# Attention and a gated expert product on one core: where unread products stand, and how late a scheduler takes results for TensorE to be

## The chip, the cores and the metric

One core of a Trainium2 chip runs the whole program in one launch. The metric is the time of one execution on the device in microseconds (us), as the median of the runs shown. Five instruction queues run beside each other: TensorE (PE in the profile; its weight loads are PEld), VectorE (DVE), ScalarE (ACT), GpSimd (POOL) and SyncE (SP), which here issues all transfers. Each queue runs its instructions in the order in which the program lists them, and waits on semaphores for what the others make.

## What is computed

The reference, cut to its core (8 batches, 8 heads, 576 positions, 64 columns of a head; d_model 512, d_ff 2048):

```python
scores = scale * q @ k.T + (cum[:, None] - cum[None, :])   # cum: running sum of log f
scores = where(causal, -1e9, scores)
attn = exp(scores - scores.max(-1)); attn /= attn.sum(-1) + 1e-9
x = (attn @ v)                       # heads side by side: 4608 tokens x 512
h = x @ w_in
g = h * tanh(softplus(h))
out = g @ w_out
```

## The kernel before

All products run with fp16 operands that are split into a high and a low part, so that one product of the reference becomes two or three on TensorE (some products of the first attention pairs run in fp32).

**Attention** goes by 32 pairs of heads, four pairs to a batch. For each pair the two operands are loaded (`qk`), scaled and split on DVE and ACT (`hl`), sent by transfers into the tiles `st1` and `st2` from which TensorE reads them, and multiplied. The first eight pairs take the row maxima first: TensorE writes scores, DVE reduces them (`mx`), the maxima are rounded (`m16`), turned on TensorE against the identity (`idh`), copied (`mr`) and sent back into `st1` as one more row. Later pairs (`new_st_items`) write scores into a bank of PSUM, DVE takes the minimum of the negated scores (`mn`), ACT takes the exponential (`st<-b,mn`), the result is split (`hb`) and turned by a transfer (`pt<-hb`), and TensorE multiplies it with the values (`b<-vv,pt`); DVE divides (`rr`, then `x<-b,rr`), splits (`xp`) and a transfer turns that into `xa`.

**Experts** go by nine chunks of 512 tokens. For each chunk TensorE forms `b<-xa,wall` (192 products of 512 columns), ACT applies the gate (`me`), DVE and ACT split it (`gh`, `gl`), and TensorE forms `b<-gh,wall` and `b<-gl,wall` (192 more). Chunk c needs the whole of batch c; the ninth chunk holds the last 64 positions of all batches. So there are 3456 products with `wall`, 384 to a chunk, and they are TensorE's filler beside the attention of the next batch. PSUM has eight banks, `b0` to `b7`. Before the experts start, attention uses all but one; from then on it has two alone (`NA = 2`, lines 909 and 1598), `b0` and `b1`, and every use of a bank waits until the last reader of the one before has left it.

**The order** of all instructions is written by a planner in the kernel's own code (class `Program`, lines 109 to 465 and on). `add` and `choose` record each operation with what it reads and writes and a cost. `schedule` (line 306) runs `forward` (line 367) ten times, each with ranks from `backward`, and keeps the order with the earliest modelled end; `emit` (line 293) writes that order out, queue by queue. `forward` is a list scheduler: it keeps a clock for each queue, takes the queue that can go first, picks the operation with the best rank whose inputs have arrived by the model, and sets when its results arrive at others: its end plus a fixed delay of its queue:

```python
DELAY = {"tensor": 197, "vector": 140, "scalar": 150, "gpsimd": 80}
```

The maps `read` and `written` hold, bank by bank, when the last reader or writer leaves it by the model. Nothing of these model times is in the program that runs: only the order is.

`forward` also places **unread products**: 128x128 products of the identity with itself into a spare part of `b7` (`emit`, the branch `i < 0`), which nothing reads. They occupy TensorE in its early gaps, so that the activity that sets its clock goes on. They are placed while `filling` holds, which ends with the first product that has `wall` as its weights. In the profile they are the line L299, `b<-idh`.

Of the kernel before, what the change touches and what calls it, by code (L numbers as in the profile page):

```python
# [26 lines left out]
P = 128  # L27
# [16 lines left out]
STAY = 10000.0  # L44
TICK = 10240.0 / 3.0
WARM = 3072.0
IDLE = 300.0
MAN = "PE"
PLO0 = ("T00", "T20", "T01", "T21",)
# [95 lines left out]
class Program:  # L145
# [221 lines left out]
    def forward(self, deps, succ, rank):  # L367
        ops = self.ops
# [5 lines left out]
        clock = {q: 0.0 for q in self.NAMES}  # L374
# [8 lines left out]
        left, half, mode = {}, 0, False  # L383

        def arrive(i):
            for o, (q, _, _, _) in enumerate(ops[i][0]):
                heappush(coming[q], (ready[i], i, o))
# [19 lines left out]
        order = []  # L407

        read, written = {}, {}
        filling, began, fills = True, False, 0  # L410
        while len(order) < n + fills:
            clock["sync"] = max(clock["sync"], hw, dma - BACK)
            best = None
            for q in self.NAMES:
# [5 lines left out]
                if r or c:  # L420
                    t = clock[q] if r else max(clock[q], c[0][0])
                    if best is None or (t, q) < best:
                        best = (t, q)
            t, q = best
# [7 lines left out]
            while ripe[q]:  # L432
# [3 lines left out]
                late = max([other.get(b, 0.0) for b in self.banks[x[1]]], default=0.0)  # L436
# [38 lines left out]
            if wait:  # L475
                heappush(ripe[q], got)
                _, i, o, t = min(wait)
# [3 lines left out]
            if way[0][1].startswith("dma_start"):  # L481
                hw = max(t, hw) + cost[0]
                clock[q] = t + 50
                dma = max(dma, hw + 650) + cost[1]
                end, own = dma + 930, 0.0
            else:
                if q == "tensor":
                    filling = filling and ops[i][0][o][1][0][3].get("lhsT", self.idle[1]).tensor.name != self.last
                    e = clock[q]
                    while filling and began and t - e > IDLE:  # L490
                        k = int((e + 197.0) / TICK)
                        e += P / (2.4 if left.get(int(e / TICK) - 1, 0.0) >= WARM else 1.2) + 2.5
                        left[k] = left.get(k, 0.0) + P
                        order.append((-1, 0))
                        fills += 1
                    began = True
                    t = max(t, e)
                    cols, weight, h, m = cost
                    if m != mode:
                        t += 97.0  # L500
                    mode = m
                    slow = 1.0 if left.get(int(t / TICK) - 1, 0.0) >= WARM else 2.0
                    cost = 22.0 if h and half and h != half else cols * slow / 2.4 + (2.5 if slow < 2 else 0.0)
                    a, b = (t + 197.0) / TICK, (t + 197.0 + cols * slow / 2.4) / TICK
                    for k in range(int(a), int(b) + 1):
                        left[k] = left.get(k, 0.0) + weight * (min(b, k + 1) - max(a, k)) / (b - a)
                    half = h
                elif lock:
                    port = max(t, port) + cost
                    cost = port - t  # L510
                elif q == "scalar" and self.sets[i] not in (None, table):
                    table = self.sets[i]
                    cost += 1370.0
                clock[q] = t + cost
                end, own = clock[q], self.DELAY[q]
            ends[i] = end
            for b in self.banks[i]:
                (written if q == "tensor" else read)[b] = end + own
            for j in succ[i]:
                d = 0.0 if q == "tensor" and ops[j][0][0][0] == q else own  # L520
                ready[j] = max(ready[j], end + d)
                need[j] -= 1
                if not need[j]:
                    arrive(j)
# [1145 lines left out]
```

## Time and profile before

| | |
|---|---|
| median of 3 runs | 1052.54 us (1052.1 to 1053.11) |
| the profiled execution | 1052.55 us, its span 1050.8 us |
| PE busy | 1009.3 us (96%), 7404 instructions |
| DVE busy | 712.9 us (68%) |
| ACT busy | 644.5 us (61%) |
| mean granted TensorE clock | 0.996 of full speed |
| DMA | 140.12 MB |

The profile is of one execution. Busy times are of instructions that do work; a waiting engine is idle. A row of the timeline gives start, length, engine, operation and tiles, how many instructions were merged, and in brackets the engine's idle time before it and what ended it. Nearly all instructions are recorded through one helper and carry its line, L302, so groups are told apart by the names of their tiles. A product of 512 columns is listed with the time from its start to its modelled end; the next one starts before that.

### The profile page before, as it was taken

To read this page: it belongs to the slowest core of one execution; us is meant where nothing else is said; L and a number is where in the kernel's file an instruction comes from. 1 tells how busy PE (TensorE), PEld (TensorE's weight loads), DVE (VectorE), ACT (ScalarE), POOL (GpSimd) and SP (SyncE) were. 2 spreads that over 40 slices of the span, in tenths; PEclk is the share of its full clock that TensorE was granted. 3 is DMA by queue.
4 is the path that set the end of the run, shared out by engine and by line. 5 is a ranking of instruction groups with operands and counts; after the bars stand their busy time and mean duration, and the time that the engine had idled before them with its cause. 6 is when DMAs were issued, how large, how long until landed. Compare 5 with 4: busy or idle time off the path is not lost.

```text
span 1050.8 us, 19908 instructions
## 1 busy us (share of the span) xinstructions
PE 1009.3 (96%) x7404; PEld 541.9 (52%) x7404; DVE 712.9 (68%) x1965; ACT 644.5 (61%) x1160; POOL 13.7 (1%) x63
## 2 busy tenths in 40 slices
PE   2899999999999999999999999999999999999998
PEld 2787566554445545445545554554455554444443
DVE  6799999867777877777777786777776663121211
ACT  5367887556777867777777767777676573112111
POOL 3000000000000000000000000000000000000000
PEclk9899999999999999999999999999999999999999
DMA  8698856548685877586767666766556332000001
GB/s 281 179 248 233 251 153 177 186 104 189 129 164 128 189 144 151 120 185 147 133 143 177 139 146 134 160 150 125 117 131 131 76 64 65 1 1 30 11 1 41
DMA packets 239340, 140.12 MB, mean 133 GB/s; under 512 B 206885, under 2 KB 207665, under 8 KB 239242
## 3 DMA queue, kind: packets, MB, share of 16 engines
q1 hardware_dynamic: 239242, 138.84, 56.9%
q8 instruction: 58, 0.95, 0.4%
q14 instruction: 40, 0.33, 0.1%
HBM read 48.33 MB, written 12.57 MB: 58 GB/s over the span
## 4 chain that ended last, share of the span: by engine, by line
PE 67%; DVE 12%; ACT 11%; DMA 5%; issue 4%; SPq 1%; ACTq 0%; POOL 0%; DVEq 0%
PE b L302 66%; ACT L302 3%; DMA st<-hl 3%; ACT st L302 2%; DVE b L302 2%; ACT hb L302 2%; ACT junk L302 2%; DVE vv L302 2%; DVE hb L302 1%; DVE hl L302 1%; ACT me L302 1%; DVE x L302 1%; DVE mx L302 1%; SPq L302 1%; DMA v<-in_v_dram 1%
## 5 line engine op out<-in xcount | busy, mean ns | idle before, releaser
L302 PEld LDWEIGHTS <-wall 128*128 128x128 f16 x3456 | 330.4, 98 | 374.6 <-issue 1.5
L302 PE MATMUL b<-xa,wall 128*128 128x512 f16 x1728 | 408.6, 379 | 0.0
L302 PE MATMUL b<-gh,wall 128*128 128x512 f16 x1152 | 356.8, 379 | 0.0
L302 PE MATMUL b<-gl,wall 128*128 128x512 f16 x576 | 218.3, 379 | 0.0
L302 ACT ACTIVATE st<-b,mn 128x512 f32<-128x512 f32 (+3 forms) x240 | 115.3, 524 | 102.1 <-DVE mn L302 90.4
L302 ACT ACTIVATE me<-b,cinv 128x512 f32<-128x512 f32 x144 | 93.1, 685 | 125.2 <-PE b L302 124.5
L302 DVE TENSOR_SCALAR gh<-me,gsc 128x512 f16<-128x512 f32 x135 | 63.7, 484 | 144.1 <-ACT me L302 140.9
L302 PE MATMUL b<-st 70*128 70x256 f16 (+12 forms) x1008 | 145.0, 278 | 12.3 <-DVE x L302 5.2
L302 ACT ACT_TABLE_LOAD x110 | 141.1, 1283 | 9.5 <-DVE mn L302 5.9
L302 DVE TENSOR_TENSOR hb<-st,hb 128x512 f16<-128x512 f32 x144 | 98.7, 690 | 62.7 <-ACT hb L302 61.9
L302 PE MATMUL b<-vv,pt 128*128 128x65 f16 (+4 forms) x2464 | 122.3, 208 | 5.7 <-ACT st L302 4.2
L302 PEld LDWEIGHTS <-st 70*128 70x128 f16 (+5 forms) x1008 | 77.4, 101 | 74.5 <-issue 33.8
L302 DVE CUSTOM_DVE_ANT_0 b<-b,mskw 128x512 f32<-128x512 f32 (+1 forms) x192 | 94.3, 499 | 27.3 <-PE b L302 21.9
L302 DVE SCALAR_TENSOR_TENSOR gl<-me,gsc,gh 128x512 f16<-128x512 f32 x144 | 102.2, 746 | 0.0
L302 ACT ACTIVATE hb<-st 128x512 f16<-128x512 f32 x144 | 89.3, 628 | 11.5 <-DMA pt<-hb 10.1
L302 PEld LDWEIGHTS <-pt 128*128 128x128 f16 (+1 forms) x2016 | 61.4, 101 | 20.4 <-issue 7.2
L302 ACT ACTIVATE junk<-qk 128x576 bf16<-128x576 f32 x64 | 43.5, 680 | 16.5 <-DMA qk<-in_qk_dram 15.6
L302 PEld LDWEIGHTS b<-vv,pt 128*128 128x128 f32 (+1 forms) x448 | 51.1, 183 | 4.5 <-issue 1.3
L302 DVE SCALAR_TENSOR_TENSOR hl<-qk,qt,hl 128x576 f16<-128x576 f32 x64 | 50.6, 810 | 0.0
L302 DVE SCALAR_TENSOR_TENSOR wall<-wall 128x512 int32<-128x512 int32 x64 | 43.1, 679 | 0.0
L302 ACT ACTIVATE xp<-x 128x128 f16<-128x128 f32 (+1 forms) x40 | 15.6, 418 | 44.0 <-DVE x L302 44.0
L302 DVE TENSOR_REDUCE mx<-b 128x1 f32<-128x384 f32 (+5 forms) x72 | 34.1, 511 | 11.9 <-PE b L302 11.7
(105 smaller groups left out, 639.1 us busy)
## 6 DMA issues: line engine op xcount, KB each, us to landing
st<-hl SPq DMA_DIRECT2D x192, 144.0 KB
qk<-in_qk_dram SPq DMA_DIRECT2D x32, 576.0 KB
v<-in_v_dram SPq DMA_DIRECT2D x32, 288.0 KB
out_dram<-ot SPq DMA_DIRECT2D x36, 256.0 KB
wall<-in_w_in_dram SPq DMA_DIRECT2D x16, 512.0 KB
wall<-in_w_out_dram SPq DMA_DIRECT2D x16, 512.0 KB
pt<-hb SPq DMA_TRANSPOSE x144
part<-ot SPq DMA_DIRECT2D x8, 256.0 KB
```

Source lines behind the costliest of these rows:

```text
L302: r = getattr(real[eng], method)(*a, **kw)
```

## The change

Two things change in `forward`, and a constant `SLACK = 600.0` (nanoseconds) is added.

First, the unread products. Before, the operation that ended a gap was appended to the order and the unread products that were to fill the gap were appended after it. Now they are inserted in front of it. The filling also stops early: past the middle of a gap, once the clock is full by the model and the activity counted so far is enough by its reckoning.

Second, once the experts run (`filling` is off), whatever VectorE, ScalarE, GpSimd or a transfer makes for TensorE, and every bank that VectorE or ScalarE has read, is taken by the model to come 600 ns later than before. Results for other engines keep their times, and so does TensorE's own work.

```diff
--- before.py
+++ after.py
@@ -44,6 +44,7 @@
 STAY = 10000.0
 TICK = 10240.0 / 3.0
 WARM = 3072.0
+SLACK = 600.0
 IDLE = 300.0
 MAN = "PE"
 PLO0 = ("T00", "T20", "T01", "T21",)
@@ -486,12 +487,17 @@
             else:
                 if q == "tensor":
                     filling = filling and ops[i][0][o][1][0][3].get("lhsT", self.idle[1]).tensor.name != self.last
-                    e = clock[q]
-                    while filling and began and t - e > IDLE:
+                    e, full = clock[q], t - IDLE
+                    while filling and began and e < full:
                         k = int((e + 197.0) / TICK)
-                        e += P / (2.4 if left.get(int(e / TICK) - 1, 0.0) >= WARM else 1.2) + 2.5
+                        warm = left.get(int(e / TICK) - 1, 0.0) >= WARM
+                        now = int((t + 197.0) / TICK)
+                        due = 1.2 * WARM * ((t + 197.0) / TICK - now)
+                        if warm and 2.0 * e > clock[q] + t and left.get(now, 0.0) > due:
+                            break
+                        e += P / (2.4 if warm else 1.2) + 2.5
                         left[k] = left.get(k, 0.0) + P
-                        order.append((-1, 0))
+                        order.insert(-1, (-1, 0))
                         fills += 1
                     began = True
                     t = max(t, e)
@@ -514,10 +520,12 @@
                 clock[q] = t + cost
                 end, own = clock[q], self.DELAY[q]
             ends[i] = end
+            late = 0.0 if q == "tensor" or filling else SLACK
             for b in self.banks[i]:
-                (written if q == "tensor" else read)[b] = end + own
+                (written if q == "tensor" else read)[b] = end + own + late
             for j in succ[i]:
-                d = 0.0 if q == "tensor" and ops[j][0][0][0] == q else own
+                to = ops[j][0][0][0]
+                d = 0.0 if q == to == "tensor" else own + late if to == "tensor" else own
                 ready[j] = max(ready[j], end + d)
                 need[j] -= 1
                 if not need[j]:
```

The new order places 164 unread products where there were 182, and otherwise the same 6967 products. Here is how it moves instructions at two places on PE.

**Place 1: PE, the end of pair 0's maxima and the begin of pair 1's.** `b2<-idh,m16` is the turn of pair 0's maxima, `b4<-st1_1` the first score product of pair 1. Before (78 unread products stand between the turn and that product, 35 more behind it):

```order
L302 MATMUL b1_0_116<-msk2_77,idm_75 128x64
L302 LDWEIGHTS m16_0_126
L302 MATMUL b2_0_118<-idh_74,m16_0_126 9x128
L299 LDWEIGHTS idh_74
L299 MATMUL b7_0_105<-idh_74 128x128
...
L302 LDWEIGHTS st1_1_82
L302 MATMUL b4_0_120<-st1_1_82 128x128
L299 LDWEIGHTS idh_74
L299 MATMUL b7_0_105<-idh_74 128x128
...
L302 LDWEIGHTS idm_75
L302 MATMUL b4_0_120<-msk_76,idm_75 128x128
```

In the change (58 stand in front of the turn, the last two of them shown; 26 between it and the product):

```order
L300 LDWEIGHTS idh_74
L300 MATMUL b7_0_105<-idh_74 128x128
L303 LDWEIGHTS m16_0_126
L303 MATMUL b2_0_118<-idh_74,m16_0_126 9x128
L300 LDWEIGHTS idh_74
L300 MATMUL b7_0_105<-idh_74 128x128
...
L303 LDWEIGHTS st1_1_82
L303 MATMUL b4_0_120<-st1_1_82 128x128
L303 LDWEIGHTS idm_75
L303 MATMUL b4_0_120<-msk_76,idm_75 128x128
```

So the gap's fill has moved ahead of the operation that waits, and behind pair 1's first product none is left. The first group of the program moves in the same way: 35 stood behind pair 0's first score product `b2<-st1_0` and now stand in front of it.

**Place 2: PE, a bank that goes from the product with the values to the scores of the next pair, in the third batch.** `b1<-vv,pt` are the last products with the values; the next user of `b1` is `b1<-st1_1 128x256`; products with `wall` stand between. Before (9 of them; the fence leaves out six):

```order
L302 MATMUL b1_0_116<-vv_0_128,pt_2_135 64x65
L302 LDWEIGHTS wall_69
L302 MATMUL b2_0_118<-xa1_87,wall_69 128x512
L302 LDWEIGHTS wall_69
L302 MATMUL b2_0_118<-xa1_87,wall_69 128x512
...
L302 LDWEIGHTS wall_69
L302 MATMUL b3_0_119<-xa1_87,wall_69 128x512
L302 LDWEIGHTS st1_1_82
L302 MATMUL b1_0_116<-st1_1_82 128x256
L302 LDWEIGHTS st2_1_85
```

In the change (14 of them):

```order
L303 MATMUL b1_0_116<-vv_0_128,pt_2_135 64x65
L303 LDWEIGHTS wall_69
L303 MATMUL b3_0_119<-xa1_87,wall_69 128x512
L303 LDWEIGHTS wall_69
L303 MATMUL b3_0_119<-xa1_87,wall_69 128x512
...
L303 LDWEIGHTS wall_69
L303 MATMUL b4_0_120<-gl_1_166,wall_69 128x512
L303 LDWEIGHTS st1_1_82
L303 MATMUL b1_0_116<-st1_1_82 128x256
L303 LDWEIGHTS st2_1_85
```

Five more products of 512 columns stand between the bank's last write and its next, and two of them are now from the second half of the experts.

## Rows read from the trace of the kernel before

**Rows 1.** The page's first part: busy time, share of the span, instructions.
```profile
PE 1009.3 (96%) x7404; PEld 541.9 (52%) x7404; DVE 712.9 (68%) x1965; ACT 644.5 (61%) x1160; POOL 13.7 (1%) x63
```

**Rows 2.** PE's waits in 0 to 98 us: total, times, longest us.
```profile
PE b L302 <- DVE am_m L302: 14.3, 1, 14.3
PE b L302 <- DVE m L302: 4.8, 1, 4.8
PE b L302 <- DMA st<-hl: 3.1, 1, 3.1
```

**Rows 3.** PE's waits in 98 to 1051 us, the same columns.
```profile
PE b L302 <- ACT st L302: 6.9, 14, 1.3
PE b L302 <- DVE x L302: 5.2, 10, 1.4
PE b L302 <- DMA pt<-hb: 0.6, 1, 0.6
PE b L302 <- ACT pt L302: 0.2, 1, 0.2
```

**Rows 4.** Timeline, 14 to 42 us, all queues, rows of several windows.
```profile
14.35 0.59 PE L302 MATMUL b<-am_m,ones 128*128 128x1 f32 x2 [14.35 <-DVE am_m L302]
14.62 3.92 SPq L302 DMA_DIRECT2D st<-hl  x6
18.01 0.26 PE L302 MATMUL b<-st 70*128 70x128 f16 x1 [3.07 <-DMA st<-hl]
18.07 3.94 PE L299 MATMUL b<-idh 128*128 128x128 f16 x35
...
21.31 0.77 ACT L302 ACTIVATE hl<-qk,qt 128x576 f16<-128x576 f32 x1 [1.65 <-DMA st<-hl]
21.80 0.30 PE L302 MATMUL b<-msk,idm 128*128 128x128 f16 x1
22.48 1.35 DVE L302 TENSOR_REDUCE mx<-b 128x4 f32<-128x512 f32 x3 [3.57 <-PE b L302]
23.75 0.51 DVE L302 TENSOR_SCALAR hl<-qk,qt 128x576 f16<-128x576 f32 x1
23.87 0.20 PE L302 MATMUL b<-msk,idm 128*128 128x64 f16 x1
24.33 4.43 SPq L302 DMA_DIRECT2D st<-hl  x6
28.62 0.18 DVE L302 TENSOR_SCALAR m<-mx 128x9 f16<-128x9 f32 x1
28.86 0.27 PE L302 MATMUL b<-idh,m 128*9 128x128 f16 x1 [4.78 <-DVE m L302]
29.06 6.01 PE L299 MATMUL b<-idh 128*128 128x128 f16 x78
31.14 0.69 DVE L302 SCALAR_TENSOR_TENSOR wall<-wall 128x512 int32<-128x512 int32 x1
34.97 2.12 PE L299 MATMUL b<-idh 128*128 128x128 f16 x35
36.92 0.22 PE L302 MATMUL b<-msk,idm 128*128 128x128 f16 x1
37.53 1.95 DVE L302 TENSOR_REDUCE mx<-b 128x4 f32<-128x512 f32 x4 [5.70 <-PE b L302]
```

**Rows 5.** Busy us by stretch: length, PE, PEld, DVE, ACT, POOL, granted clock, DMA share, GB/s.
```profile
24.20:28.90 4.70, 0.04 (x1) 0.04 (x1) 4.67 (x14) 0.35 (x2) 0.00 (x0) 0.62 0.77 212
24.10:38.90 14.80, 9.54 (x134) 9.18 (x135) 9.04 (x26) 1.84 (x5) 0.24 (x1) 0.77 0.70 218
38.90:100.20 61.30, 60.28 (x615) 49.70 (x615) 56.12 (x169) 39.82 (x91) 1.03 (x7) 1.00 0.84 217
```

**Rows 6.** Timeline of PE and DVE, 244 to 248 us (place 2).
```profile
244.15 2.12 PE L302 MATMUL b<-xa,wall 128*128 128x512 f16 x9
246.92 0.42 DVE L302 TENSOR_TENSOR x<-b,rr 128x256 f32<-128x256 f32 x1
247.26 0.34 DVE L302 TENSOR_SCALAR x<-b,rr 128x128 f32<-128x128 f32 x1
247.65 0.60 PE L302 MATMUL b<-st 70*128 70x256 f16 x4 [1.39 <-DVE x L302]
```

**Rows 7.** Instructions that write `b`: count, ns min/median/max, first and last start, forms.
```profile
L302 PE MATMUL b<-xa,wall x1728: 376/379/390, 100.2 to 1035.8; 128*128 128x512 f16 x192
```

**Rows 8.** Busy us by stretch, one batch and the end, columns as in rows 5.
```profile
425.00:534.00 109.00, 106.09 (x830) 54.17 (x830) 82.48 (x232) 80.40 (x144) 0.56 (x4) 1.00 0.72 150
857.00:1047.00 190.00, 189.56 (x955) 87.11 (x954) 47.58 (x91) 41.91 (x64) 0.00 (x0) 1.00 0.07 21
```

**Rows 9.** The chain that ended last, two of its pieces: start, length, what.
```profile
642.60 38.39 PE b L302 x340
...
856.95 189.63 PE b L302 x955
```

## Prediction, made before the changed kernel ran

> **What bounds the kernel now.** I read the page's first part first: PE is busy 96% of the span, DVE 68%, ACT 61% [rows 1]. The chain of waits agrees: it runs on PE alone for 38 us in the middle of a batch and for the last 190 us [rows 9]. So only time in which PE does no useful product can be won: the 41.5 us in which it is idle (1050.8 less 1009.3), and what the profile counts as busy although nobody reads it. The waits of PE divide the idle time. Before 98 us it waits three times for long: 14.3 us for its first operand, 3.1 us for a transfer, 4.8 us for the rounded maxima [rows 2]. After 98 us it waits 26 times, 12.9 us in all, mostly for an ACT or DVE operation that reads one of the two banks of attention [rows 3]. A wait costs more than its row says: a 512-column product is listed with 379 ns [rows 7], while nine of them in 2.12 us start (2.12 - 0.379)/8 = 0.218 us apart [rows 6]; so about 0.16 us of each wait lies under the end of the product before. 26 times 0.16 is 4.2 us, and the waits after 98 us cost about 17.1 us.
>
> **Part one, the unread products.** The timeline of the start shows what they do now [rows 4]. The first score product of pair 0 runs at 18.01, when its transfer has landed. Then come 35 unread products, to 21.80, and only then the rest of pair 0's scores, whose operand is the same tile. DVE sits idle 3.57 us for that. The turn of the maxima runs at 28.86, 78 unread products follow to 34.9, one score product of pair 1, then 35 more, to 36.92; DVE sits idle 5.70 us until 37.53. PE was not short of ready work: pair 1's operands were being sent from 24.33 on, and the first such transfer of pair 0, issued at 14.62 and needed at 18.01, took at most 3.4 us, so they were there by about 28.
>
> Step by step in the change. The first 35 start behind the product that ends at 14.94. At (3.94 - 0.25)/34 = 0.108 us each they end at 18.7, 0.7 us later than pair 0's operand arrives. The other 26 products of pair 0, which took from 21.80 to 24.07, then run from 18.75 to 21.0, 3.05 us sooner. DVE's three reductions move to about 19.4 and end by 20.8. Its next step, the split of pair 1, needs the buffer that transfers still read: ACT's half of that split started at 21.31 for that reason. So DVE's block from 23.75 to 28.80, 5.05 us all but without a gap [rows 4, 5], starts at 21.3 and ends at 26.35: 2.45 us sooner, not 3.05. Before the turn stand 58 unread products: at (2.12 - 0.22)/34 = 0.056 us each they need 3.2 us of the 5.3 us there, so they cost nothing; at 0.108 they would end at 27.3 and cost 0.9. Then 26 more, 1.5 us (2.8 at the lower clock). Pair 1's scores start at about 28 to 29.2 and go through without a break, where 36.92 was. DVE has 3.0 us of other work behind the maxima (28.80 to 31.83), so it reduces from about 29.5, not 37.53: **8 us** sooner.
>
> How much of that lasts? From 38.9 to 100.2 us PE is busy 60.28 of 61.3 us, DVE 56.12, transfers 0.84 [rows 5]: all three are nearly full, so each has to start this stretch sooner. PE and DVE can, by 8. The transfers between 24.1 and 38.9 are busy 0.70 of 14.8 us, so they have 4.4 us of idle time to give, and are issued 2.4 us sooner: 6.8. I take 6, and take off 0.5 us for three later groups, 12, 19 and 5 products, where 25 stood, if their gaps are not there on the chip (11 times 0.056). Sum -5.5; ends -2 (only the 2.45 us of the maxima, less the fills) and -9 (DVE's whole idle time, 3.57 and 5.70).
>
> The granted clock is 0.77 between 24.1 and 38.9 [rows 5], part of it at 1.2 GHz after the idle stretch ahead of 28.86. With 58 products in that stretch the lower level should be gone there; what that gives back is in the steps above.
>
> **Part two, 600 ns.** Where PE waits now, the order should have more work in front of the waiting operation. At place 2, DVE leaves the bank at 247.60, and PE has waited 1.39 us after nine products [rows 6]; now 14 stand there, so 5 times 0.218 is 1.09 of the 1.39 + 0.16 us. I looked up the 25 longest of these waits in both orders: 17 have more products with `wall` in front, most of them three to five (0.65 to 1.1 us), three have 18 or 19 more; four have as many as before, four have fewer. 17 of 25 of 17.1 us is 11.6. I take 11, since a product that is moved forward is missing elsewhere. Ends: -3, if the operations that wait are merely late somewhere else, and -17, if all waits go.
>
> What pays for the fill? The products with `wall` that remain after the last attention product: 806 of 3456 before, 802 now. The interleave as a whole keeps its pace; attention is not drawn out in the order. The stretch at the end runs PE 189.56 of 190 us [rows 8] and stays. ACT and DVE have 29 and 27 us to spare in a batch of 109 [rows 8], so work that leaves them later is still done in time.
>
> **The sum.** The profiled execution took 1052.55 us (span 1050.8), the median is 1052.54, so no correction is needed. 1052.5 - 5.5 - 11 = **1036 us**.
>
> **A rule that speaks against it.** The waits come back batch after batch at the same kind of place, where a bank passes from DVE or ACT to PE [rows 3]. The Trainium skill, Perfetto Trace Analysis, section Optimization Strategy, says that a gap which repeats on the engine that should be full can mean that too few buffers are there. By that rule two banks would be the limit, and no order would remove the waits: the sum would be 1052.5 - 5.5 - 1 = 1046. Against it stands that ACT and DVE are idle a quarter of the batch [rows 8] and PE alone carries the chain for 38 us of it [rows 9]: a bank limit that held throughout would leave no such stretch.
>
> **Rivals.**
> 1. The waits only move (the bank limit): front gain alone, 1046 us. For it: 4 of 25 places have fewer products in front. Chance 0.15.
> 2. The front gain is eaten before 210 us by DVE and transfers, which are nearly full there: 1052.5 - 0.5 - 11 = 1041 us. For it: DVE's 56.12 of 61.3 us. Chance 0.13.
> 3. Slower. Each of the 24 pairs from the ninth on uses an attention bank nine times, 216 uses on two banks, 108 in a row. If PE comes 0.6 us late to each, because the products put in front outlast the real wait, attention is drawn out by 65 us. The reserve is small: 806 less the 768 products of the last two chunks, 38 times 0.218 = 8 us. If half of the hand-overs are late so, it is 1052.5 - 5.5 + 32 - 8 = 1071 us; it turns slower once over (8 + 5.5)/65, a fifth, are. Against it: after a late hand-over PE has done useful work, and the idle time of ACT and DVE takes it up. Chance 0.05.
> 4. Both parts give and take nothing, because the order is a new one everywhere and has new waits of its own: 1052 us. Chance 0.04.
>
> **How the numbers follow.** My forecast has 0.63, with 1028 to 1041 of its own. The range goes up to rivals 1 and 2 and the lower ends of both parts (1052.5 - 2 - 3 = 1047.5) and down towards the upper ends (1026.5): 1028 to 1047. Faster by over 0.2% (2.1 us, about what a measurement of this kernel can tell from no change) is the forecast with rivals 1 and 2, 0.91, less a little for a mixture: 0.90; same 0.05; slower 0.05.
>
> **What would show it.** Right: pair 1's scores in one piece before 30 us, DVE's idle time for PE gone at 22.5 and 37.5, the first `wall` product 5 to 6 us sooner than at 100.2 [rows 7], PE's waits after 98 us at 4 us or less by the row, the end stretch still about 190 us. Wrong: the first `wall` product at 99 us or later (rival 2), waits for `st` and `x` still near 12 us (rival 1), or a longer time without products with `wall` on PE and a shorter end stretch (rival 3).

## The result, and the profile after

| | before | changed |
|---|---|---|
| median of 13 runs each, side by side | 1052.67 us (1051.76 to 1057.64) | 1058.37 us (1039.12 to 1078.65) |
| the profiled execution | 1052.55 us, span 1050.8 | 1056.15 us, span 1054.3 |
| its mean granted TensorE clock | 0.996 | 0.980 |

The ratio is 0.9915 [0.9894, 0.9937], which is 1043.7 us; it leaves out executions more than 1.5% above their kernel's fastest, eight of the thirteen here, so the median over all of them stands beside it. By the ratio the change is faster, and 1043.7 lies in the predicted range of 1028 to 1047. By the median of all runs it is 5.7 us slower, and only three of the thirteen executions lie in the range.

What orders the thirteen is the clock. Those with a mean granted clock of 0.997 or 0.998 took 1039.12, 1041.01 and 1042.46 us; 0.991 and 0.989 took 1047.43 and 1050.97; 0.976 to 0.980, five of them, 1056.15 to 1062.21; 0.966 took 1070.39; 0.959 and 0.960 took 1076.87 and 1078.65. So the kernel gains 10 to 14 us where the clock holds, and gives it back where it does not. The profiled execution is one of the middle group. The page of it, first the busy times, then the clock that was granted in 40 slices of the span:

```profile
PE 1022.0 (97%) x7386; PEld 551.9 (52%) x7386; DVE 698.8 (66%) x1940; ACT 659.8 (63%) x1187; POOL 13.4 (1%) x63
...
PEclk9579899999999999999999999999999999999999
```

PE is busier than in [rows 1], by 12.7 us, and yet the execution is 3.6 us longer: products at half clock count as busy. Before, no slice's digit was under 8; now there are a 5 and a 7 in the second and third slice, 26 to 79 us. The timeline of the changed kernel from 14 to 34 us, to be held against [rows 4]:

```profile
14.83 3.54 PE L300 MATMUL b<-idh 128*128 128x128 f16 x35
...
19.50 1.35 DVE L303 TENSOR_REDUCE mx<-b 128x4 f32<-128x512 f32 x3
20.34 3.40 PE L300 MATMUL b<-idh 128*128 128x128 f16 x58
...
22.08 4.58 SPq L303 DMA_DIRECT2D st<-hl  x6
...
25.87 0.22 PE L303 MATMUL b<-idh,m 128*9 128x128 f16 x1 [2.13 <-DVE m L303]
26.03 1.62 PE L300 MATMUL b<-idh 128*128 128x128 f16 x26
29.82 0.22 PE L303 MATMUL b<-st 70*128 70x128 f16 x1 [2.17 <-DMA st<-hl]
30.48 2.42 DVE L303 TENSOR_REDUCE mx<-b 128x4 f32<-128x512 f32 x5
```

Until 30 us it went as the steps said: the maxima of pair 0 reduced at 19.50 instead of 22.48, the turn at 25.87 instead of 28.86, pair 1's scores at 29.82 and its reductions at 30.48 instead of 37.53. Pair 1's transfers (SPq, 22.08) are issued 2.25 us sooner than at 24.33, and PE now waits for one of them. Then the clock goes. Busy time by stretch (columns as in [rows 5]):

```profile
24.10:31.50 7.40, 3.46 (x53) 3.11 (x54) 5.74 (x18) 1.60 (x5) 0.24 (x1) 1.00 0.72 204
31.50:65.60 34.10, 34.10 (x200) 26.10 (x198) 19.46 (x54) 15.00 (x36) 0.32 (x3) 0.50 0.71 206
65.60:106.60 41.00, 40.04 (x411) 33.83 (x410) 38.56 (x120) 23.10 (x53) 0.44 (x4) 1.00 0.77 196
...
98.00:200.00 102.00, 97.30 (x681) 61.55 (x681) 98.42 (x289) 75.95 (x146) 0.48 (x4) 0.97 0.66 186
200.00:857.00 657.00, 652.43 (x5034) 336.27 (x5033) 475.30 (x1344) 488.94 (x861) 3.20 (x23) 1.00 0.68 144
857.00:1050.00 193.00, 193.00 (x976) 88.64 (x974) 49.77 (x98) 43.28 (x68) 0.00 (x0) 1.00 0.08 23
...
106.60:110.00 3.40, 3.40 (x19) 1.75 (x18) 3.40 (x7) 2.56 (x7) 0.00 (x0) 0.50 0.91 266
```

From 31.5 to 65.6 us TensorE runs at 1.2 GHz, without a moment of idle time: 34.10 of 34.10 us busy, in 200 products; in the 41.0 us behind it, at 2.4 GHz, it does 411. Before, it ran at that level too, but from 25.4 to 32.2 us alone:

```profile
25.40:32.20 6.80, 3.34 (x31) 3.23 (x32) 6.37 (x19) 1.34 (x3) 0.24 (x1) 0.50 0.57 136
...
98.00:200.00 102.00, 101.75 (x713) 62.83 (x714) 100.00 (x290) 79.94 (x153) 0.37 (x3) 1.00 0.68 196
200.00:857.00 657.00, 643.69 (x4955) 328.73 (x4954) 486.31 (x1359) 467.88 (x824) 3.20 (x23) 1.00 0.67 141
```

(That fence is the kernel before, in stretches of its own.) Two short falls of about 3.4 us, at 106.6 and 123.7, are new as well. PE's waits of the changed kernel from 98 us on (total us, times, longest; the first three in 98 to 200 us, the last in all the rest):

```profile
PE b L303 <- DVE mx L303: 2.9, 5, 1.0
PE b L303 <- DMA st<-mr: 0.9, 1, 0.9
PE b L303 <- DVE mr L303: 0.7, 1, 0.7
...
PE b L303 <- ACT st L303: 4.3, 9, 1.2
```

Behind 200 us 12.7 us of waits for `st`, `x` and `pt` [rows 3] have become 4.3, and none for `x` is left, that of place 2 [rows 6] among them. From 98 to 200 us it is the other way: 0.2 us before, all of it for `pt`, and 4.5 now. The order is not all that the 600 ns change: the planner also gives operations to another engine, so that DVE has 1940 instead of 1965 and ACT 1187 instead of 1160. The products that write `b` from `xa` and `wall` (count, ns min/median/max, first and last start):

```profile
L303 PE MATMUL b<-xa,wall x1728: 376/379/634, 109.2 to 1039.3; 128*128 128x512 f16 x192
```

That splits the profiled difference of 3.5 us of span: the first product with `wall` comes 9.0 us later than at 100.2 [rows 7], and from there to the end it takes 945.1 us where it took 950.6, 5.5 less. The chain of waits at the end is longer on PE alone: 257.68 us in one piece, where it was 189.63 [rows 9]. Between 98 and 200 us the chain now runs on DVE's work on `wall` for 38.4% of the stretch, where it was 0.6%.

```profile
132.46 2.14 DVE wall L303 x4
134.67 3.08 DVE wall L303 x6
...
792.34 257.68 PE b L303 x1499
```

Two things had to be explained: why the clock falls for so long near the start, and what the 600 ns do before 200 us.

### The profile page after: what moved, and what is told of

It reads as the page before. It is cut to its first block, busy times and chain, and to the rows that moved or that the text cites. A ratio compares the mean times of both kernels' runs of the same rounds, so it can differ in the third digit from the quotient of the medians.

```text
span 1054.3 us, 19917 instructions
## 1 busy us (share of the span) xinstructions
PE 1022.0 (97%) x7386; PEld 551.9 (52%) x7386; DVE 698.8 (66%) x1940; ACT 659.8 (63%) x1187; POOL 13.4 (1%) x63
## 4 chain that ended last, share of the span: by engine, by line
PE 71%; DVE 14%; ACT 7%; issue 4%; DMA 3%; SPq 0%; ACTq 0%; DVEq 0%
PE b L303 70%; DVE wall L303 4%; ACT st L303 2%; DVE b L303 2%; DVE hb L303 2%; DMA st<-hl 2%; ACT L303 2%; ACT hb L303 1%; DVE gl L303 1%; ACT junk L303 1%; DVE mx L303 1%; DVE hl L303 1%; ACT me L303 1%; DVE vv L303 1%; DVE x L303 1%
## 5 line engine op out<-in xcount | busy, mean ns | idle before, releaser
L303 PE MATMUL b<-st 70*128 70x256 f16 (+12 forms) x1008 | 154.4, 290 | 10.6 <-ACT st L303 3.6
L303 DVE TENSOR_SCALAR gh<-me,gsc 128x512 f16<-128x512 f32 x120 | 57.2, 481 | 144.5 <-ACT me L303 142.7
L303 PE MATMUL b<-vv,pt 128*128 128x65 f16 (+4 forms) x2464 | 127.2, 212 | 0.8 <-ACT st L303 0.7
L303 PEld LDWEIGHTS <-st 70*128 70x128 f16 (+3 forms) x1008 | 81.1, 105 | 72.0 <-issue 28.2
L303 DVE CUSTOM_DVE_ANT_0 b<-b,mskw 128x512 f32<-128x512 f32 (+1 forms) x192 | 93.6, 502 | 15.8 <-PE b L303 13.3
L303 PEld LDWEIGHTS b<-vv,pt 128*128 128x128 f32 (+1 forms) x448 | 56.8, 201 | 3.4 <-ACT pt L303 0.2
L303 ACT ACTIVATE pt<-b 128x512 f32<-128x512 f32 x48 | 27.6, 594 | 25.0 <-PE b L303 24.3
L303 DVE TENSOR_SCALAR rr<-b 128x4 f32<-128x4 f32 (+1 forms) x64 | 10.2, 159 | 42.8 <-PE b L303 42.6
```

The costliest lines, as they stand in the source:

```text
L303: r = getattr(real[eng], method)(*a, **kw)
```

## The experiments

Each was timed in five rounds beside the kernel before, whose medians there were 1052.76 to 1053.18 us. e1 to e4 ran on one chip, e5 to e8 on a second, e9 to e11 on a third, e12 on a fourth, so runs of different groups are compared through the kernel before. "Fallen" counts the executions whose mean granted clock is under 0.985; over some 1050 us that is more than 31 us at 1.2 GHz. The "late stretch" is that in which the 600 ns are taken.

| run | unread products | late stretch | median (range, executions) us | ratio | fallen |
|---|---|---|---|---|---|
| changed | in front | experts on | 1058.37 (1039.12 to 1078.65, 13) | 0.9915 [0.9894, 0.9937] | 8 |
| e1_front_only | in front | none | 1056.19 (1046.86 to 1076.08, 12) | 1.0001 [0.9976, 1.0026] | 6 |
| e2_slack_only | behind | experts on | 1050.22 (1047.59 to 1053.21, 12) | 0.9974 [0.9960, 0.9987] | 0 |
| e3_after_behind | behind | experts on | 1049.48 (1046.24 to 1063.39, 12) | 0.9972 [0.9950, 0.9995] | 1 |
| e4_after_filled | in front, more | experts on | 1057.58 (1055.45 to 1073.9, 9) | 1.0045 [1.0025, 1.0065] | 7 |
| e5_slack_late | behind | from 200 us | 1039.74 (1039.64 to 1040.54, 4) | 0.9873 [0.9854, 0.9891] | 0 |
| e6_front_guarded | in front, more | none | 1059.39 (1044.72 to 1076.91, 12) | 0.9947 [0.9920, 0.9974] | 6 |
| e7_banks_only | behind | experts on, banks | 1051.17 (1048.18 to 1068.64, 12) | 0.9982 [0.9969, 0.9994] | 1 |
| e8_results_only | behind | experts on, results | 1053.3 (1049.62 to 1074.68, 12) | 0.9999 [0.9985, 1.0013] | 1 |
| e9_front_late | in front | from 200 us | 1040.34 (1037.66 to 1050.09, 6) | 0.9891 [0.9857, 0.9926] | 1 |
| e10_front_delayed | in front, 100 more | none | 1048.3 (1045.64 to 1065.09, 13) | 0.9957 [0.9938, 0.9975] | 2 |
| e11_slack_1200 | behind | from 200 us, 1200 ns | 1048.21 (1047.03 to 1060.04, 12) | 0.9968 [0.9941, 0.9996] | 0 |
| e12_late_delayed | in front, 100 more | from 200 us | 1041.99 (1037.88 to 1057.05, 12) | 0.9900 [0.9873, 0.9926] | 2 |

### The two parts alone

**e1_front_only**: the kernel before with its 182 unread products placed in front. All other products keep their order.

```diff
-                        order.append((-1, 0))
+                        order.insert(-1, (-1, 0))
```

> The order of before with all its 182 unread products, each group moved in front of the operation that ends its gap; no 600 ns. Theory C (what spreads the changed kernel's times is TensorE's clock, which falls when the engine is idle ahead of pair 1's scores and then stays low through the attention products; the fills behind the operation, however late they made it, had kept it up): pair 1's scores start near 30 us, 6 to 7 us sooner than before; executions whose clock stays take 1045 to 1048 us, and some others, with a mean clock under 0.99, take 1055 or more. Rival O (the new order of the other products, not the place of the fills, brings the clock down): mean clock 0.995 or more in every execution, 1045 to 1048 us.

Measured: no gain, and six fallen executions of twelve. The six others took 1046.86 to 1053.24 us. So the long falls come with this part alone. In the profiled execution (1059.13 us) the fall comes at another time than in the changed kernel, though. The timeline of PE shows what it waited for last:

```profile
59.50 0.19 PE L302 MATMUL b<-st 71*64 71x64 f16 x1 [0.30 <-DMA st<-mr]
```

Busy time of the same kernel by stretch:

```profile
52.90:59.80 6.90, 6.60 (x68) 5.91 (x67) 6.87 (x23) 4.09 (x10) 0.00 (x0) 1.00 1.15 255
59.80:94.00 34.20, 34.20 (x202) 26.30 (x201) 19.85 (x58) 14.28 (x30) 0.33 (x3) 0.50 0.62 169
```

Ahead of this fall PE was busy 6.60 of 6.90 us at the full clock, and waited 0.30 us for a transfer of `mr`, the maxima sent back. Then 34.2 us at half clock follow, again without idle time. The first product with `wall` comes at 106.6 us.

**e2_slack_only**: the kernel before with the 600 ns alone.

```diff
+SLACK = 600.0
+            late = 0.0 if q == "tensor" or filling else SLACK
-                (written if q == "tensor" else read)[b] = end + own
+                (written if q == "tensor" else read)[b] = end + own + late
-                d = 0.0 if q == "tensor" and ops[j][0][0][0] == q else own
+                to = ops[j][0][0][0]
+                d = 0.0 if q == to == "tensor" else own + late if to == "tensor" else own
```

> The 600 ns alone: the changed kernel's order of all products that are read, with the unread ones behind the operation that ends a gap, as before (183 of them). Theory C: the clock is low for some 7 us after 25 us and then holds in every execution, mean 0.995 or more; the waits of PE after 98 us fall from 12.9 to 3 to 5 us, time 1040 to 1045 us, spread under 4 us. Rival O: times spread as in the changed kernel, from 1039 to 1078 us, with mean clocks down to 0.96.

Measured: 2.6 us gained, no execution fallen. That is far from 11, and from the 1040 to 1045 us that theory C expected. (The program holds 199 unread products, not the 183 of the expectation; the products that are read stand in the changed kernel's order.) PE's waits (the first three in 98 to 200 us, the last in the rest; columns as above):

```profile
PE b L303 <- DMA st<-hl: 2.2, 1, 2.2
PE b L303 <- DVE mx L303: 1.9, 3, 1.0
PE b L303 <- DVE mr L303: 0.7, 1, 0.7
...
PE b L303 <- ACT st L303: 5.4, 11, 2.1
```

And busy time in the two stretches:

```profile
98.00:200.00 102.00, 96.93 (x651) 59.28 (x649) 99.42 (x294) 78.34 (x152) 0.37 (x3) 0.97 0.63 183
200.00:857.00 657.00, 651.33 (x5029) 335.39 (x5028) 472.00 (x1329) 488.07 (x857) 3.24 (x23) 1.00 0.69 143
```

Behind 200 us PE is busy 7.6 us more than before; from 98 to 200 us it is busy 4.8 us less and does 62 products fewer, with the clock down for 3.4 us at 124.1 and at 185.6. The profiled execution, 1052.66 us, is 2.4 us above this kernel's median. The gain and the loss are in two stages of one part.

**e3_after_behind**: the changed kernel, its unread products written out behind the operation that ends their gap.

```diff
-        order = self.schedule(deps)
+        order, held = [], 0
+        for x in self.schedule(deps):
+            if x[0] < 0:
+                held += 1
+            else:
+                order += [x] + [(-1, 0)] * held
+                held = 0
```

> The changed kernel with its own 164 unread products, each group put behind the operation that ends its gap. Theory C: with 58 and 26 behind the turn and behind pair 1's first score product, PE is back at real work by about 33 to 35 us, and the clock comes back as before: mean 0.994 or more, 1040 to 1045 us, little spread. A rival within C (the number, not the place, keeps the clock): spread of 10 us or more with clocks under 0.985. Rival O: spread as in the changed kernel.

Measured: with every other instruction in the changed kernel's order, one fallen execution of twelve instead of eight of thirteen, and a median 8.9 us lower, though not the 1040 to 1045 us of theory C. With e1 against e2 (six of twelve against none, on one chip) this shows that the place of the unread products makes the long falls frequent.

**e4_after_filled**: theory C, that the idle time ahead of 25.87 and 29.82 us starts the fall: the groups of 58 and 26 become 90 and 70, all in front.

```diff
+        order, held, most = [], 0, [90, 70]
+        for x in self.schedule(deps):
+            if x[0] < 0:
+                held += 1
+                continue
+            if held > 9 and held != 35 and most:
+                held = most.pop(0)
+            order += [(-1, 0)] * held + [x]
+            held = 0
```

> The changed kernel with 90 unread products where it has 58 (in front of the turn of pair 0's maxima) and 70 where it has 26 (in front of pair 1's first score product), so that PE is busy through both waits up to 30 us. Theory C: the clock does not fall at 31 us in any execution, mean 0.996 or more, 1037 to 1041 us, faster than before and than the changed kernel in all executions. Rival O: mean clock still under 0.985 in half of the executions, 1055 us or more there.

Measured: theory C does not explain the falls. Seven of nine executions fell, and none held a mean clock of 0.990. The gaps are full in the profile, and there is indeed no fall at 31 us there, but one as long came later, at 62.9 us, behind a wait for `mr`, as the timeline of PE shows:

```profile
20.58 5.19 PE L308 MATMUL b<-idh 128*128 128x128 f16 x90
25.98 4.08 PE L308 MATMUL b<-idh 128*128 128x128 f16 x70
...
62.93 0.21 PE L311 MATMUL b<-st 71*64 71x64 f16 x1 [2.08 <-DMA st<-mr]
```

Busy time by stretch:

```profile
62.90:97.00 34.10, 34.07 (x202) 26.37 (x201) 20.51 (x57) 13.83 (x30) 0.22 (x2) 0.50 0.66 181
```

### Where the 600 ns help, and which half of them

**e5_slack_late**: theory S, that the first stage behind the start has nothing to win, and that the 600 ns belong to the time after it. They are taken from 200 us on by the model; the unread products stand behind, as before.

```diff
+LATE = 200000.0
-            late = 0.0 if q == "tensor" or filling else SLACK
+            late = 0.0 if q == "tensor" or filling or t < LATE else SLACK
```

> The 600 ns only where the model's clock is past 200 us, the unread products behind the operation as before. Theory S (the 600 ns take away waits of PE where attention has two banks, after 200 us, and make new ones between 98 and 200 us, where DVE is full and maxima and transfers feed PE): PE waits under 1 us between 98 and 200 us, about 5 us after 200 us, 1041 to 1045 us, mean clock 0.995 or more. Rival N (the new waits come with any new order, wherever the 600 ns apply): 1048 to 1052 us, with 3 us of waits or more between 98 and 200 us.

Measured: 1039.74 us, ratio 0.9873 [0.9854, 0.9891], the four executions within 0.9 us of each other at clocks of 0.996 to 0.998. This is the best kernel of the study by its median, 13 us under the kernel before and faster than theory S had it. Four executions are few: a fall in one of ten or so is not excluded. The first line of its page's busy times, to be held against [rows 1]:

```profile
PE 1006.2 (97%) x7406; PEld 542.6 (52%) x7406; DVE 696.9 (67%) x1936; ACT 660.1 (64%) x1189; POOL 13.8 (1%) x63
```

PE is busy 3.1 us less than before, and 15.8 us less than in the changed kernel's profile. Its products from `xa` and `wall`:

```profile
L304 PE MATMUL b<-xa,wall x1728: 376/379/390, 100.7 to 1023.0; 128*128 128x512 f16 x192
```

PE's waits, the first two in 98 to 200 us, the last behind:

```profile
PE b L304 <- DVE mx L304: 0.7, 2, 0.4
PE b L304 <- DVE x L304: 0.2, 1, 0.2
...
PE b L304 <- ACT st L304: 2.2, 7, 0.5
```

And busy time in the two stretches, 10.5 us more than before behind 200 us and 0.75 less from 98 to 200:

```profile
98.00:200.00 102.00, 101.00 (x709) 62.78 (x709) 99.54 (x291) 78.55 (x150) 0.37 (x3) 1.00 0.70 193
200.00:857.00 657.00, 654.23 (x5045) 336.04 (x5044) 477.87 (x1349) 495.90 (x871) 3.22 (x23) 1.00 0.68 143
```

From the first product with `wall` to the end it takes 1038.0 - 100.7 = 937.3 us, 13.3 less than the kernel before. Against e2 the profiled spans differ by 12.9 us; 0.9 of it is the first product with `wall` (101.6 there), 3.9 the waits in 98 to 200 us (4.8 there, 0.9 here), 3.2 those behind (5.4 and 2.2), 3.4 the two short falls of 3.4 us at half speed: 11.4 of the 12.9.

**e7_banks_only** and **e8_results_only**: e2 with half of the 600 ns each, for freed banks or for results alone.

```diff
e7: -                d = 0.0 if q == to == "tensor" else own + late if to == "tensor" else own
    +                d = 0.0 if q == to == "tensor" else own
e8: -                (written if q == "tensor" else read)[b] = end + own + late
    +                (written if q == "tensor" else read)[b] = end + own
```

> The 600 ns for freed banks alone, unread products behind. If the waits after 200 us go by banks that are read late (ACT st and DVE x end most of them), they fall to 4 to 6 us as with both; between 98 and 200 us fewer new waits than with both, since maxima and transfers keep their times: 1045 to 1049 us. If results matter as much: waits after 200 us stay at 8 us or more and the time at 1050 to 1053.

> The 600 ns for results alone (what DVE, ACT and transfers make for TensorE), freed banks as before, unread products behind. By the theory that the waits after 200 us go by banks: waits for ACT st and DVE x after 200 us stay at 8 to 12 us, 1050 to 1054 us. By the other: they fall to 6 us or less, 1043 to 1049 us.

Measured: behind 200 us e7 waits 4.7 us and e8 7.6, where e2 waits 5.4 and the kernel before 12.7; from 98 to 200 us 4.7 and 4.3, against 4.8 and 0.2. PE's waits behind 200 us, the longest two rows of e7, then of e8:

```profile
PE b L303 <- ACT st L303: 3.2, 7, 0.8
PE b L303 <- DVE x L303: 1.3, 5, 0.5
...
PE b L303 <- ACT st L303: 6.0, 14, 1.5
PE b L303 <- DVE x L303: 1.6, 3, 0.8
```

So freed banks alone take away as much of the late waits as both halves together, results alone less (5.1 of 12.7), and each half alone pays about the whole price of the early stage. By the times e7 (0.9982) and e2 (0.9974) cannot be told apart, and e7 stayed above the 1045 to 1049 us expected of it; e8 gains nothing. e7 also settles a question that e2 and e5 leave: there the 600 ns move operations from DVE to ACT as well (in e5 DVE has 1936 instead of 1965, ACT 1189 instead of 1160), but in e7 DVE has 1973 and ACT 1154, and the late waits fall all the same.

**e11_slack_1200**: e5 with twice the delay.

```diff
-SLACK = 600.0
+SLACK = 1200.0
```

> The 600 ns past 200 us made 1200 ns, fills behind. If 600 ns already cover nearly all waits (2.2 us of them were left by the rows), it gains 1 to 2 us at most: 1037.5 to 1039.5 us. If a late hand-over of attention's two banks draws attention out, as the slower rival had it, it loses: 1043 us or more, with fewer products with wall left after the last attention product and PE waits near the end.

Measured: 8.5 us slower than e5. Waits behind 200 us are 7.8 us instead of 2.2, 2.8 of them for the gate (`me`), which none of the profiles above shows. Another 2.6 us already stand at the first product with `wall`, at 103.3 instead of 100.7: the order differs ahead of 200 us too. After the last attention product 794 products with `wall` are left, where e5 has 802 and the kernel before 806.

### What makes the clock fall

**e6_front_guarded**: e1 with ten more unread products ahead of the first 64-row score product of each of the first eight pairs, the one that waited in e1 at 59.50 and in e4 at 62.93. Theory G has it that this wait starts the fall.

```diff
+            kw = ops[i][0][o][1][0][3]
+            if "lhsT" in kw and tuple(kw["lhsT"].shape) == (KM, D) and int(kw["out"].shape[0]) == D:
+                thin += 1
+                for _ in range(10 * (thin % 2)):
+                    real["tensor"].matmul(out=self.idle[0], lhsT=self.idle[1], rhs=self.idle[1], start=True, stop=True)
```

> The order of before with its unread products in front, and 10 unread products more ahead of the smallest score products (64 by 64) of each of the first eight pairs, which follow the fp32 products with the values; each ten cost 0.56 us where nothing waits. Theory G (with PE ahead of the transfers, the clock falls where PE waits there, and a fall among attention's products lasts 34 us): the clock holds through 50 to 100 us, no execution with a mean clock under 0.985, 1046 to 1052 us. Rival H (the clock falls from the fp32 and small products themselves as soon as they are drawn together, fill or not): executions of 1056 to 1078 us in the same share as without the ten, a third or more.

Measured: six fallen of twelve, as e1. So that wait is not the only cause, or ten products do not cover it; the share of falls gives theory G no support. The profiles speak for it in part: the long falls of e1, e4 and e10 (below) begin at 59.8, 62.9 and 68.8 us, within 0.6 us of one and the same product, the first 64-row score product of the third pair, which waited for `mr` in all three; in the profiles of e6, e9 and e12, all with the unread products in front, nothing waits there, and no fall begins there. Where the fallen executions of e6 fell is not on record. Where the clock held, as in the profiled execution (1047.71 us, 0.998), the first product with `wall` is at 96.2 us.

**e10_front_delayed**: theory R, that PE, started sooner, runs ahead of the transfers and of DVE and meets gaps there: e1 with 100 more unread products right behind pair 1's first score product, so that it starts sooner but goes on later.

```diff
+        order, held, groups = [], 0, 0
+        for x in self.schedule(deps):
+            order.append(x)
+            if x[0] < 0:
+                held += 1
+            elif held:
+                held, groups = 0, groups + 1
+                if groups == 3:
+                    order += [(-1, 0)] * 100
```

> The order of before with its unread products in front, and 100 more unread ones behind pair 1's first score product, which make PE 5.6 us later again. Theory R: PE is late against its feeders as before, the clock holds, no execution with a mean clock under 0.99, 1049 to 1053 us. Rival P (the place in front itself brings the clock down, not that PE is early): as with the fills in front alone, a third or more of the executions at clocks under 0.985 and 1059 us or more.

Measured: two fallen of thirteen, eleven at 0.995 or more, and 4.9 us less than the kernel before by the medians. Giving PE useless work at this place made the kernel faster than e1 by 7.9 us. Both the delay and the added activity are new there, and no run separates them; in its profile a fall that began at 31.3 us, among these products, was over after 3.4 us (shown with e9 below). It does not remove the falls: the profiled execution (1065.09 us) had one, behind waits of 0.90 us for `pt` and 0.32 us for `mr` in the timeline of PE:

```profile
65.12 2.60 PE L310 MATMUL b<-vv,pt 128*128 128x65 f32 x22 [0.90 <-ACT pt L310]
68.29 0.19 PE L310 MATMUL b<-st 71*64 71x64 f16 x1 [0.32 <-DMA st<-mr]
```

Busy time by stretch, ahead of the fall and in it:

```profile
61.90:68.80 6.90, 5.68 (x58) 5.04 (x57) 5.79 (x18) 3.37 (x8) 0.00 (x0) 1.00 1.01 212
68.80:103.00 34.20, 34.20 (x200) 26.39 (x200) 19.74 (x57) 14.54 (x30) 0.33 (x3) 0.50 0.58 168
```

**e9_front_late** and **e12_late_delayed**: do the two gains add? e9 is the changed kernel with the 600 ns from 200 us on (the edit of e5; it holds 154 unread products); e12 is e5 with the edits of e1 and e10.

> The changed kernel with its 600 ns only past 200 us of the model's clock: the same order of all products that are read as in the run with the 600 ns late and the fills behind, but its unread products (155) stand in front. Theory R (fills behind made PE late against the engines that feed it, so that it always had work; put in front, PE catches up with them, waits, and its clock falls): executions spread by 15 us or more with mean clocks down to 0.98 or less; where the clock holds, 1031 to 1035 us. Rival: the spread came from the waits which the 600 ns made before 200 us, so without them the clock holds in every execution, 1031 to 1035 us throughout.

> The order of the run with the 600 ns past 200 us, with its unread products in front and 100 more behind pair 1's first score product, as in the run that delayed PE again. If the two effects add (5 us from the start, as the delayed run had it where the clock held, and 13 us from the late 600 ns): 1033 to 1037 us in most executions, faster than both kernels and than the late 600 ns alone. If PE's early clock and its later waits depend on each other: 1039 us or more, or a third of the executions over 1050 us.

Measured: they do not. Both reach 1037.66 and 1037.88 us at best, 2 us under e5, with the first product with `wall` at 96.8 and 97.5 us in the profiles. But they spread over 12 and 19 us, and their medians, 1040.34 and 1041.99, are no better than e5's 1039.74. No execution of e9 reached the 1031 to 1035 us that both sides expected where the clock holds. In e9's profile the clock fell at the place of the changed kernel's long fall too, but for 10.2 us; in e6's and e10's it fell there for 3.4 us, and in e12's not at all. Busy time by stretch, of e9, e6 and e10:

```profile
31.40:41.60 10.20, 10.20 (x68) 6.78 (x66) 6.61 (x18) 4.97 (x11) 0.37 (x1) 0.50 0.92 263
31.50:34.90 3.40, 3.40 (x25) 2.25 (x23) 3.06 (x7) 0.77 (x1) 0.00 (x0) 0.50 0.81 245
31.30:34.70 3.40, 3.40 (x36) 3.40 (x34) 0.00 (x0) 0.78 (x1) 0.00 (x0) 0.50 0.86 259
```

Over all runs: with the unread products in front 28 of 52 executions fell (the changed kernel, e1, e4, e6, e9), with them behind 3 of 64 (e2, e3, e5, e7, e8, e11), with 100 more behind pair 1's first product 4 of 25, and of the kernel before beside the experiments 1 of 101. The border cuts close: two executions of e11 and one of e3, at 0.985, are not counted but took 1059.91 to 1060.04 us, 10 to 12 us over their medians. With 0.985 included it is 30 of 52, 6 of 64, 4 of 25 and 1 of 101, and the order stays.

## Why the prediction was right, and where it was not

The time by the ratio, 1043.7, lies in the range, and faster had 0.90. That is in part luck: 1043.7 rests on the five executions in which the clock fell least, and nothing in the sum foresaw that the other eight would lie outside the range. The sum of 1036 is 8 us off even so, and two of its steps failed.

**Part one, the start: right to 30 us.** Pair 1's scores came at 29.82 (forecast 28 to 29.2) in one piece but for the nine unread products at its end, DVE reduced from 30.48 (forecast 29.5). DVE's idle time for PE at 22.48 and 37.53 is gone. Of 8 us sooner 7.05 came. One term was short: the prediction let a transfer take at most 3.4 us, and in the changed kernel's chain the one that pair 1's scores wait for took 5.79 (24.03 to 29.82).

**Part one, "How much of that lasts?": the step that failed.** It took 6 of the 8 us as lasting, with transfers as the limit. Its neighbour was worse: "With 58 products in that stretch the lower level should be gone there". The stretch at 1.2 GHz did not go; it moved from 25.4 to 32.2 us to 31.5 to 65.6 us and became five times as long. I had looked for the clock only in the idle stretch that the unread products were to fill, not behind it, where PE now goes on 7 us sooner while pair 1's transfers are issued 2.25 us sooner. The clock as a way in which the change could lose was missing among the rivals. By e1 and e3 the place of the unread products makes such falls frequent; by e4 the idle time at 24 to 30 us is not needed for them, since without it they came all the same, in the profile at another place. With the 100 products of e10 they are fewer (4 of 25 in e10 and e12) without ending: this fits that PE runs ahead of what feeds it, as do the three long falls that begin at one wait for `mr`, but it is not shown, and the trigger stays open.

What the first part is worth at a held clock is 5 to 8 us alone (e10: -4.9 by the median; the five executions of e6 at 0.998 or more took 1044.72 to 1047.71 us), where -5.5 was forecast, but 2 us at best on top of e5. The first product with `wall` then comes at 96.2 to 97.5 us, 3 to 4 sooner and not 5 to 6 (e6, e9 and e12). Rival 2, that the front gain is eaten before 210 us, describes the outcome (before to e1, e5 to e9: nothing gained by the median), but not its cause as given: DVE is busy 19.46 of the 34.10 us in the long fall, and transfers 0.71. It is the clock.

**Part two, the sum: right in kind, wrong in where.** "17 of 25 of 17.1 us is 11.6. I take 11" is what the 600 ns give when they are taken from 200 us on: e5 gains 13.0 us, waits after 98 us go from 12.9 us in 26 to 3.1 in 10. By the prediction's own rule for the hidden part of a wait that is 9.8 + 16 times 0.16 = 12.4 us. The mechanism is shown: with the same two banks the waits go when the order has more products in front, and by e7 they go without work moving from DVE to ACT. Counted in the orders, from the last product on the bank to the one that waited, 24 of the 25 waits behind 200 us can be matched, and in e5, as in the changed kernel, 22 of them have more products with `wall` in front and two have fewer, where the prediction had counted 17 of 25.

What failed is that the prediction took 98 to 1051 us as one stretch, and [rows 3] as its account. The waits in 98 to 200 us were 0.2 us of the 12.9: nothing was to be won there. DVE was busy 100.00 of 102 us in that stretch, and in the changed kernel's chain above DVE's work on `wall` is on the path there. There the same 600 ns made 4.5 us of new waits, with short falls of the clock beside them. The price is e2 against e5, 10.5 us, which is most of the gain. That the row "4 us or less after 98 us" came out as 8.8 shows this step wrong.

**The cover and the end: right.** After the last attention product 802 products with `wall` are left, the end stretch is busy 193.00 of 193 us.

**The rivals of part two.** Rival 1, too few banks, fell by e5: the bank waits went without another bank. So the rule of the Trainium skill that was weighed against the change (Perfetto Trace Analysis, section Optimization Strategy: a repeating gap can mean too few buffers) does not hold for these gaps, with 12.9 us of them before and 3.1 after. Rival 3, attention drawn out, did not come at 600 ns. At 1200 ns 8.5 us are lost and PE waits for the gate, but the number of products left at the end, 794, hardly moved: that this loss is rival 3 is not shown.

## What to carry to other kernels

Give the scheduler's model a margin only where the profile shows waits to be won: list them by stage first, since the same 600 ns gained 13 us in one stage and cost 10 in the one before it. Before an in-order engine is made to start sooner, ask whether what feeds it comes sooner as well; if not, the gap can move behind the start, and in these runs the clock then fell more often, for a reason that they leave open. Repeat the timing and read each execution's granted clock: one execution of the changed kernel, at 0.998 or at 0.960, would have told one of two opposite stories.

## What was not expected of the hardware

A fall of the clock among attention's small products lasted 34.1 to 34.2 us in four kernels (the changed one, e1, e4, e10), although PE was busy through all of it, and 10.2 us in e9, from the same place as in the changed kernel. It lasted 3.4 us where unread products filled most or all of it (e6 at 31.5, e10 at 31.3), and among or just ahead of the products of 512 columns (the changed kernel at 106.6 and 123.7, e2 at 124.1 and 185.6). So a busy PE does not by itself get its clock back soon; what in the kinds of work decides it no run here isolates. The price of one long fall can be read from the changed kernel's executions: 1056.15 us at 0.980 against 1039.12 at 0.998 is 17 us, 1.6%. The Trainium skill, TensorE: Matmul & The Clock Gate, Part 1, section What's actually happening, puts the cost of the ramp under 1% of a typical kernel's span. That is said of the ramp, the slow products with which a kernel begins; a fall later in the kernel, as here, costs more, and 1078.65 us at 0.960 is 3.8% over 1039.12.
